# A long convolution with a period of 22912 in place of 23168, ahead of two gated layers

## The chip, the cores and the metric

The kernel runs on one core of a Trainium2 chip. The metric is device time in microseconds (us). Three runs of the kernel before took 1347.17, 1348.60 and 1349.86 us; the median is 1348.6 us.

## The reference

The program computes a long convolution along the sequence, gates it with its input, and sends the result through two feed-forward layers. Cut to what matters:

```python
# x, v: (1, 12480, 128); pos_emb: (12480, 64)
h_filt = (np.maximum(pos_emb @ w1, 0) @ w2) * np.exp(-0.01 * pos)[:, None]
u = x * v
y = irfft(rfft(u, n=2 * S) * rfft(h_filt, n=2 * S))[:S]      # S = 12480, a causal convolution
x = x * y
h = x @ w_in;   x = (h * clip(h + 3, 0, 6) / 6) @ w_out       # d_ff = 2048
h = x @ w_in2;  out = where(h > 0, h, exp(min(h, 0)) - 1) @ w_out2
```

The window `exp(-0.01 n)` is zero in float32 from n = 10398 (`ZERO`) on, so a circular convolution of any period of at least 12480 + 10398 - 1 = 22877 gives the wanted outputs.

## The kernel before, in words

The period is `L = N1 * N2` with `N1 = 180` and `N2 = 128`. A Fourier transform of that length is done in two steps, one along n1 (98 blocks of 128 tokens are not zero) and one along n2; since the data are real, `NK = N1 // 2 + 1 = 91` frequencies along n1 are kept. Everything up to the gate is float32 matrix multiplication against tables that are loaded from memory. In the trace a float32 multiplication appears as two matmul instructions. The work has these stages, one after the other on TensorE (PE):

1. *Hidden filter* (`filter_hidden`, line 278): `pos_emb @ w1`, its two-fold sums into `qb`.
2. *First step* (`first`, lines 320 to 327): 32 blocks of four signal columns and 16 blocks of four filter columns, interleaved two to one. For each block eight multiplications write a PSUM tile `pa` of which 2·NK columns per signal column are used (182 before); the two folds `f` run beside each other on two halves of the output partitions. ScalarE (ACT) evicts each block in one instruction, line 327, into `Au` (a signal half in `qb`, the other in `au`, laid out `(d, k, r)` so that the pitch of one channel is 2·NK elements, 728 bytes) or into `Ar`.
3. *Second step* (lines 378 to 417): the frequencies go in octets of eight (`OCTETS`), eleven full ones and a last one of `NK % 8`, 3 before. For each frequency there is one multiplication `r` (`second_r`), two `h` side by side (`second_h`) and two `z`, one for each half of the channels (`second_u`). VectorE (DVE) then makes two products (line 411) in the buffers `m1` and `m2`, two sets in turn, and GpSimd (POOL) adds them into `Au` (line 416). `z` reads `Au` as its moving operand: 64 pairs of neighbouring floats, one channel pitch apart. Beside this, one job after another of converting int64 weights (lines 198 to 215, over ACT, DVE and POOL) is slipped in by `convert`. The last three octets do their first halves together, then their second halves.
4. *Third step* (`third`, lines 424 to 431): blocks of four channels (the last three of the second half are shorter); eight multiplications each into a PSUM tile `q`, one ACT copy (line 429), two DVE instructions (line 431). The weight operand has NK columns.
5. *Fourth step* (`fourth`, line 504): 33 steps with a table `ti` of NK partitions loaded just ahead (line 472, five buffers), each followed by a DVE product with the signal `xp` (line 549), which had been loaded into `au` in pieces of `EX * 2 * NK` columns (lines 475 to 492).
6. *The two layers* (lines 604 to 698): 25 token tiles of 512, in float32r with a high and a low part, from about 271 us on. This is three quarters of the time.

The order of each engine's instructions is the order in which the code is written; nothing reschedules it. PSUM in stages 1 to 5 is one pool `ps` with two tags, `px` and `py`, of two buffers each (`bank`, line 109). So a new tile waits until the tile two before it under the same tag has been read. Around the step from stage 3 to stage 4 the uses of `py` are, in order: `z` of the last octet's first half, `z` of the last octet but one's second half, the first block of stage 4, the third block of stage 4.

```python
KGROUPS = groups([KC] * (NK // KC) + [NK % KC])       # line 259
OCTETS = groups([OCT] * (NK // OCT) + [NK % OCT])     # line 260
```

Of the kernel before, what the change touches and what calls it, by code (L numbers as in the profile page):

```python
# [9 lines left out]
F32 = mybir.dt.float32  # L10
# [8 lines left out]
S, D, FO, FF = 12480, 128, 64, 2048  # L19

ZERO = 10398
N1, N2 = 180, 128
L = N1 * N2
H1 = -(-S // N2)
NK = N1 // 2 + 1
# [5 lines left out]
HD = D // 2  # L31
# [12 lines left out]
EX = 8  # L44
# [15 lines left out]
def tables():  # L60
    n1, k1, k2 = np.arange(H1), np.arange(NK), np.arange(N2)
    i, m, a = np.arange(HN), np.arange(NM), np.arange(H1) - 2 * SHIFT - 1
    w = 2 * np.pi * (np.outer(n1 - SHIFT, k1) % N1) / N1
    c, s = np.cos(w), np.sin(w)

    t1 = np.stack([np.stack([c, -s], axis=2), np.stack([-s, -c], axis=2)], axis=1)
    k = k1[:, None] + N1 * k2
    w = np.pi * (((2 * i + 1)[:, None, None] * k) % (2 * L)) / L
    gm = np.concatenate([np.cos(w), np.sin(w)], axis=0)

    w = 2 * np.pi * (np.outer(k2, m) % N2) / N2
    c, s = np.cos(w), np.sin(w)
    cs = np.stack([
        np.concatenate([c[:, :HN], s[:, 1:HN], c[:, HN:]], axis=1),
        np.concatenate([c[:, :1], s[:, 1:HN], c[:, 1:]], axis=1),
    ], axis=1)
    ends = (m == 0) | (m == HN)
    w = 2 * np.pi * np.outer(k1, m) / L - np.where(ends, np.pi / 4, 0.0)
    w = 2 * np.pi * (np.outer(k1, a) % N1)[:, None] / N1 + w[:, :, None]
    c = np.outer(np.where((k1 == 0) | (k1 == N1 // 2), 1.0, 2.0) / L, np.where(ends, np.sqrt(0.5), 1.0))  # L80
    ti = np.stack([np.cos(w), -np.sin(w)], axis=2) * c[:, :, None, None]
    window = np.exp(-0.01 * np.arange(S, dtype=np.float32))
    assert not window[ZERO:].any()
    rows = t1 * np.exp(-0.01 * N2 * n1)[:, None, None, None]
    column = np.tile(np.exp(-0.01 * (HN + i)), 2)[:, None]
    ratio = np.tile(np.repeat(RATIO, 2), (H1, 1))
    return [np.ascontiguousarray(z, dtype=np.float32) for z in (t1, gm, cs, ti, rows, column, ratio)]
# [9 lines left out]
def tile_kernel(ctx, tc, xc, vc, xT, posT, w1_d, w2_d, moe_w, t1_d, gm_d, cs_d, ti_d, rows_d, column_d, ratio_d, outT):  # L97
# [21 lines left out]
    AW = 2 * NK * HD  # L119
    RF = FO * N2  # L120

    au = ctx.enter_context(tc.tile_pool(name="aup", bufs=1, side="right")).tile([128, 2 * NK * (HD + EX)], F32, name="au")
    zeros = au[:, -N2:]
    nc.vector.memset(zeros, 0.0)
    bounds = keep.tile([128, 2], F32, name="bounds")
# [326 lines left out]
    ends = range(last - 2, last + 1)  # L452
# [294 lines left out]
```

## Time and profile before

| what | value |
|---|---|
| median of three runs | 1348.6 us (1347.17 to 1349.86) |
| profiled execution, span from first to last instruction | 1346.2 us |
| PE, matmul busy | 1338.7 us, 99% |
| DVE / ACT / POOL busy | 1149.3 / 992.9 / 394.4 us |
| mean granted TensorE clock | 1.000 |

The profiled execution is told by its span alone; its own time is the span and the launch around it, which the page does not time apart. The median of the runs lies 2.4 us above the span. The share of busy PE time is modelled at the ends of instructions, so that a short wait of PE can hide in it; the starts of the engine that reads PE's results, ACT above all, show such a wait better.

### The profile page before, as it was taken

How to read it: one execution, taken by the hardware profiler on the slowest of the kernel's cores; microseconds unless marked ns; L12 is line 12 of the kernel's file. 1: busy time of each engine (PE TensorE's matmuls, PEld its weight loads, DVE VectorE, ACT ScalarE, POOL GpSimd, SP SyncE). 2: the span in 40 equal slices, each digit the busy share in tenths (PEclk: the TensorE clock that was granted, in tenths of full speed). 3: DMA queues.
4: the chain of work that ended last, by engine and by line, in shares of the span. 5: the costliest groups of instructions: out<-in, count | busy, mean ns of one | idle time of the engine just before them, and what ended most of it. 6: DMA issues, size and time to landing. Idle time of an engine off the chain costs nothing.

```text
span 1346.2 us, 20841 instructions
## 1 busy us (share of the span) xinstructions
PE 1338.7 (99%) x8154; PEld 1148.0 (85%) x8154; DVE 1149.3 (85%) x1230; ACT 992.9 (74%) x1171; POOL 394.4 (29%) x280
## 2 busy tenths in 40 slices
PE   9999999999999999999999999999999999999998
PEld 9999999978888888888888888888888888888898
DVE  6749887799988888888888888888888888888897
ACT  5666633288788877788778878887778877887876
POOL 1027721215322222332222232222233222222223
PEclk9999999999999999999999999999999999999999
DMA  8924319730000000000000000000000000000000
GB/s 268 258 75 142 100 34 293 237 106 1 8 0 9 8 9 9 1 8 9 9 0 9 9 9 1 8 9 9 9 1 8 9 9 1 9 8 9 9 3 17
DMA packets 32490, 58.15 MB, mean 43 GB/s; under 512 B 3879, under 2 KB 12168, under 8 KB 32392
## 3 DMA queue, kind: packets, MB, share of 16 engines
q1 hardware_dynamic: 25192, 48.11, 11.7%
q10 hardware_dynamic: 7200, 8.72, 2.0%
q8 instruction: 64, 1.05, 0.3%
q14 instruction: 34, 0.28, 0.1%
HBM read 46.23 MB, written 10.58 MB: 42 GB/s over the span
## 4 chain that ended last, share of the span: by engine, by line
PE 90%; DVE 5%; issue 2%; ACT 1%; POOL 1%; DMA 1%; SPq 0%; POOLq 0%; DVEq 0%; ACTq 0%
PE h L624 37%; PE o L668 37%; PE pa L324 4%; PE q L424 4%; PE y L504 3%; PE z L397 1%; DVE gs L658 1%; PE pr L278 1%; DVE bp L411 1%; DVE qb L411 1%; PE r L378 1%; PE h L387 1%; DVE cv L210 1%; DVE g L645 1%; DMA qb<-in_posT 0%
## 5 line engine op out<-in xcount | busy, mean ns | idle before, releaser
L668 PE MATMUL o<-gs,w 128*128 128x512 f32 (+1 forms) x2400 | 567.1, 384 | 0.5 <-DVE gs L658 0.3
L668 PEld LDWEIGHTS o<-gs,w 128*128 128x128 f32 x2400 | 445.3, 188 | 88.6 <-DVE gs L658 0.8
L637 POOL TENSOR_SCALAR a<-a 128x1024 f32<-128x1024 f32 (+1 forms) x200 | 294.5, 1472 | 720.0 <-ACT a L636 720.0
L658 DVE TENSOR_TENSOR gs<-g,gs 128x1024 fp32r<-128x1024 f32 (+1 forms) x400 | 482.4, 1206 | 4.5 <-ACT gs L653 3.7
L653 ACT CAST gs<-g 128x1024 fp32r<-128x1024 f32 (+1 forms) x400 | 410.2, 1025 | 54.4 <-DVE g L645 52.8
L645 DVE SCALAR_TENSOR_TENSOR g<-a,h 128x1024 f32<-128x1024 f32 (+1 forms) x200 | 238.6, 1193 | 121.4 <-ACT a L634 121.3
L624 PE MATMUL h<-xs,w 128*128 128x512 f32 (+1 forms) x1200 | 302.1, 387 | 0.4 <-DVE g L645 0.4
L624 PE MATMUL h<-x,w 128*128 128x512 f32 (+1 forms) x1200 | 299.0, 385 | 0.2 <-ACT a L636 0.2
L636 ACT ACTIVATE a<-h 128x1024 f32<-128x1024 f32 (+1 forms) x200 | 201.3, 1006 | 92.7 <-PE h L624 91.5
L624 PEld LDWEIGHTS h<-xs,w 128*128 128x128 f32 x1200 | 223.6, 188 | 48.5 <-DVE g L645 1.4
L624 PEld LDWEIGHTS h<-x,w 128*128 128x128 f32 x1200 | 223.0, 188 | 43.8 <-issue 0.5
L634 ACT ACTIVATE a<-h,bounds 128x1024 f32<-128x1024 f32 (+1 forms) x200 | 218.9, 1095 | 51.8 <-PE h L624 51.6
L647 DVE SCALAR_TENSOR_TENSOR g<-a,h 128x1024 f32<-128x1024 f32 (+1 forms) x200 | 237.2, 1186 | 0.2 <-POOL a L637 0.2
L215 POOL TENSOR_TENSOR cv<-cv 128x256 int32<-128x256 int32 x32 | 23.3, 729 | 96.4 <-DVE cv L212 89.8
L416 POOL TENSOR_TENSOR qb<-qb,bp 128x1024 f32<-128x1024 f32 (+2 forms) x14 | 27.7, 1981 | 71.2 <-DMA qb<-in_gm 70.7
L504 PE MATMUL y<-ti,qb 91*64 91x98 f32 (+1 forms) x1024 | 45.9, 247 | 0.8 <-DVE cv L212 0.5
L504 PEld LDWEIGHTS y<-ti,qb 91*64 91x64 f32 x1024 | 45.4, 138 | 1.3 <-DVE cv L212 0.7
L324 PE MATMUL pa<-tab,cv 98*64 98x182 f32 x512 | 44.5, 318 | 0.0
L324 PEld LDWEIGHTS pa<-tab,cv 98*64 98x64 f32 x512 | 37.6, 137 | 3.9
L198 ACT ACTIVATE cv<-cv 128x256 f32<-128x256 f32 x32 | 14.3, 447 | 35.1 <-DMA cv<-in_mw 16.8
L411 DVE TENSOR_TENSOR qb<-z,qb 128x1024 f32<-128x1024 f32 (+2 forms) x15 | 15.9, 1060 | 17.9 <-ACT qb L390 15.2
L431 DVE TENSOR_TENSOR qb<-q,au 91x512 f32<-91x512 f32 (+2 forms) x44 | 26.4, 650 | 3.8 <-ACT au L429 3.8
(67 smaller groups left out, 832.5 us busy)
## 6 DMA issues: line engine op xcount, KB each, us to landing
uv<-in_xc SPq DMA_DIRECT2D x32, 196.0 KB
out_T<-y SPq DMA_DIRECT2D x23, 256.0 KB
au<-in_xT SPq DMA_DIRECT2D x8, 728.0 KB
qb<-in_gm SPq DMA_DIRECT2D x22, 256.0 KB
ti<-in_ti SPq DMA_DIRECT2D x32, 139.3 KB
cv<-in_mw ACTq DMA_DIRECT2D x17, 256.0 KB
uv<-in_vc SPq DMA_DIRECT2D x22, 196.0 KB
w_scratch<-cv ACTq DMA_DIRECT2D x32, 128.0 KB
```

The costliest lines, as they stand in the source:

```text
L324: nc.tensor.matmul(pa[f * HN:(f + 1) * HN, j, :2 * NK], lhsT=src(j, f), rhs=table[:, f], start=True, stop=True)
L424: nc.tensor.matmul(q[:NK, r, j], lhsT=Au[hf][:, s0 + j, :, r], rhs=cs[:, r * N2:(r + 1) * N2], start=True, stop=True)
L504: nc.tensor.matmul(y[h * HD:(h + 1) * HD, off:off + w], lhsT=Q[:NK, h, j // 2, :, j % 2], rhs=ti[:, m - m0, r, H1 - w:], start=r == 0, sto ...
L624: nc.tensor.matmul(h[:, j], lhsT=wslice(2 * m - 2, a, 2 * u + j), rhs=x[:, b], start=i == 0, stop=i == 2)
L634: nc.scalar.activation(a, h, AF.Relu, bias=three)
L636: nc.scalar.activation(a, h, AF.Exp)
L637: nc.gpsimd.tensor_scalar(a, a, 1.0, 0.0, op0=ALU.min, op1=ALU.max)
L645: nc.vector.scalar_tensor_tensor(g, a, 6.0, h, op0=ALU.min, op1=ALU.mult)
L647: nc.vector.scalar_tensor_tensor(g, a, -1.0, h, op0=ALU.add, op1=ALU.max)
L653: nc.scalar.copy(t[:, 0], g)
L658: nc.vector.tensor_tensor(out=t[:, 1], in0=g, in1=t[:, 0].bitcast(F32), op=ALU.subtract)
L668: nc.tensor.matmul(o[:, :WID[t]], lhsT=wslice(2 * m - 1, a, 2 * u + j), rhs=gs[:, b, j], start=u == 0 and j == 0 and i == 0, stop=u == NU ...
```

## The change

`N1` is 179 in place of 180, so the period is 179 · 128 = 22912 and NK is 90 in place of 91. N1 is now odd, so only frequency 0 has no mirror image; the weight of a frequency in `tables` is written for either parity. The buffer `au` is sized by what it must hold beside the frequencies (`S + 4 * N2` = 12992 columns, before 2·91·72 = 13104).

```diff
 ZERO = 10398
-N1, N2 = 180, 128
+N1, N2 = 179, 128
 L = N1 * N2
 H1 = -(-S // N2)
 NK = N1 // 2 + 1
@@
-    c = np.outer(np.where((k1 == 0) | (k1 == N1 // 2), 1.0, 2.0) / L, np.where(ends, np.sqrt(0.5), 1.0))
+    c = np.outer(np.where(2 * k1 % N1 == 0, 1.0, 2.0) / L, np.where(ends, np.sqrt(0.5), 1.0))
@@
-    au = ctx.enter_context(tc.tile_pool(name="aup", bufs=1, side="right")).tile([128, 2 * NK * (HD + EX)], F32, name="au")
+    au = ctx.enter_context(tc.tile_pool(name="aup", bufs=1, side="right")).tile([128, S + 4 * N2], F32, name="au")
```

No instruction changes its place. What changes is shapes and a few counts. On PE, at the end of stage 3 and the start of stage 4 (`r`, `h`, `z` are the multiplications of stage 3, `q` those of stage 4; one row counts multiplications, each of which is two instructions in the trace):

```order
-L378 MATMUL r<-qb 128x128 x11
+L378 MATMUL r<-qb 128x128 x10
 L387 MATMUL h<-qb 128x128 x16
 L397 MATMUL z<-qb 128x128 x8
-L387 MATMUL h<-qb 128x128 x6
-L397 MATMUL z<-qb 128x128 x3
-L397 MATMUL z<-au,qb 128x128 x19
-L424 MATMUL q<-cs,qb 91x128 x128
-L424 MATMUL q<-cs,au 91x128 x128
+L387 MATMUL h<-qb 128x128 x4
+L397 MATMUL z<-qb 128x128 x2
+L397 MATMUL z<-au,qb 128x128 x18
```

One `r`, two `h` and two `z` are gone, all from the last octet, which has two frequencies now; the `q` rows go on with 90 in place of 91. On DVE, at the same place, the products of that octet are shorter and stand where they stood:

```order
-L411 TENSOR_TENSOR qb<-z,qb 128x3x64x2
-L411 TENSOR_TENSOR bp<-z,qb 128x3x64x2
+L411 TENSOR_TENSOR qb<-z,qb 128x2x64x2
+L411 TENSOR_TENSOR bp<-z,qb 128x2x64x2
 L411 TENSOR_TENSOR qb<-z,bp 128x8x64x2
 L411 TENSOR_TENSOR bp<-z,bp 128x8x64x2
 L411 TENSOR_TENSOR qb<-z,qb 128x8x64x2
 L411 TENSOR_TENSOR bp<-z,qb 128x8x64x2
```

In stage 2 all 384 multiplications `pa` have 180 moving columns, and the ACT evictions 720 elements in place of 728. The channel pitch in `Au` is 720 bytes. The 33 loads of `ti` have 90 partitions, the pieces of `xp` are 1440 columns with a last one of 960 (before 1456 and 832), and the last group of the table `gm` has two frequencies in place of three. Stage 6 is the same, instruction for instruction.

## Rows read from the trace of the kernel before

**Rows 1.** The page: busy time of the engines, and the chain that ended last.

```profile
PE 1338.7 (99%) x8154; PEld 1148.0 (85%) x8154; DVE 1149.3 (85%) x1230; ACT 992.9 (74%) x1171; POOL 394.4 (29%) x280
...
PE 90%; DVE 5%; issue 2%; ACT 1%; POOL 1%; DMA 1%; SPq 0%; POOLq 0%; DVEq 0%; ACTq 0%
```

**Rows 2.** Busy time of each engine by stretch, stages 2 to 6.

```profile
core 0: us, PE busy (x) PEld busy (x) DVE busy (x) ACT busy (x) POOL busy (x), PEclk, DMA share, GB/s
19.40:79.00 59.60, 59.60 (x768) 53.64 (x768) 43.51 (x99) 38.32 (x49) 1.16 (x2) 1.00 0.86 242
79.00:168.06 89.06, 88.27 (x912) 84.62 (x912) 69.67 (x87) 56.12 (x77) 57.86 (x36) 1.00 0.32 98
168.06:224.50 56.44, 56.20 (x514) 55.86 (x512) 49.23 (x87) 22.75 (x45) 10.07 (x9) 1.00 0.45 141
224.50:271.00 46.50, 45.90 (x1025) 45.49 (x1025) 33.08 (x78) 12.10 (x29) 12.84 (x16) 1.00 0.80 240
271.00:320.00 49.00, 48.40 (x207) 38.07 (x207) 46.26 (x43) 43.21 (x51) 11.62 (x9) 1.00 0.23 70
320.00:1330.00 1010.00, 1009.75 (x4522) 840.90 (x4521) 888.20 (x801) 803.55 (x850) 292.57 (x198) 1.00 0.02 7
```

**Rows 3.** Timeline of ACT in stage 2: start, length, instruction, [idle before <- releaser].

```profile
22.09 0.78 ACT L327 ACTIVATE qb<-pa 128x728 f32<-128x728 f32 x1 [0.47 <-PE pa L324]
23.67 0.87 ACT L327 ACTIVATE qb<-pa,column 128x728 f32<-128x728 f32 x1 [0.80 <-PE pa L324]
...
79.17 0.78 ACT L327 ACTIVATE au<-pa 128x728 f32<-128x728 f32 x1 [0.46 <-PE pa L324]
```

**Rows 4.** Who waited for whom: us in total, times, longest us.

```profile
ACT qb L327 <- PE pa L324: 14.7, 32, 1.1
...
DVE cv L269 <- PE pa L324: 7.5, 9, 0.9
```

**Rows 5.** Groups by line, stage 3: busy us, mean ns of one | idle before.

```profile
L387 PE MATMUL h<-qb 64*128 64x128 f32 x364 | 24.0, 279 | 0.4 <-ACT qb L379 0.4
L397 PE MATMUL z<-qb 128*128 128x128 f32 x182 | 23.9, 282 | 0.3 <-DVE bp L411 0.3
...
L397 PE MATMUL z<-au,qb 128*128 128x128 f32 x182 | 22.8, 277 | 0.0
L378 PE MATMUL r<-qb 128*128 128x128 f32 x182 | 22.1, 276 | 0.0
```

**Rows 6.** Timeline of ACT, the first five blocks of stage 4.

```profile
170.00 0.58 ACT L429 COPY tab<-q 91x512 f32<-91x512 f32 x1 [5.80 <-PE q L424]
171.75 0.58 ACT L429 COPY au<-q 91x512 f32<-91x512 f32 x1 [1.17 <-PE q L424]
173.64 0.58 ACT L429 COPY au<-q 91x512 f32<-91x512 f32 x1 [1.31 <-PE q L424]
175.43 0.58 ACT L429 COPY tab<-q 91x512 f32<-91x512 f32 x1 [1.21 <-PE q L424]
177.18 0.58 ACT L429 COPY au<-q 91x512 f32<-91x512 f32 x1 [1.17 <-PE q L424]
```

**Rows 7.** Timeline of DVE, the end of stage 3.

```profile
164.68 0.69 DVE L411 TENSOR_TENSOR bp<-z,qb 128x512 f32<-128x512 f32 x1
165.31 0.56 DVE L411 TENSOR_TENSOR qb<-z,qb 128x384 f32<-128x384 f32 x1
...
166.84 1.23 DVE L411 TENSOR_TENSOR qb<-z,bp 128x1024 f32<-128x1024 f32 x1 [0.49 <-POOL qb L416]
...
170.26 1.24 DVE L411 TENSOR_TENSOR bp<-z,qb 128x1024 f32<-128x1024 f32 x1
```

**Rows 8.** Timeline of POOL, the end of stage 3.

```profile
165.52 2.30 POOL L416 TENSOR_TENSOR qb<-qb,bp 128x512 f32<-128x512 f32 x2 [0.24 <-PE z L397]
...
166.76 1.06 POOL L416 TENSOR_TENSOR qb<-qb,bp 128x384 f32<-128x384 f32 x1
```

**Rows 9.** What the DMA queue of SP waited for: us in total, times, longest.

```profile
SPq L472 <- PE y L504: 20.1, 22, 2.2
```

## The prediction

> **What bounds the kernel now.** I read the page first, then the table by stretches, then the timelines of the engines that wait for PE. The page says that PE is busy 99% of the span and carries 90% of the chain that ended last [rows 1]. By stretches it is the same in every stage: 59.60 of 59.60 us in stage 2, 88.27 of 89.06 in stage 3, 56.20 of 56.44 in stage 4, 45.90 of 46.50 in stage 5, and 1009.75 of 1010.00 in most of stage 6; the granted clock is 1.00, the upper of its two levels (2.4 GHz), in all of them [rows 2]. So time can only go where PE's own work goes. But busy PE time has modelled ends, so I check at two places whether a wait of PE hides in it, by the spacing of the ACT instructions that read PE's results.
>
> The change leaves stage 6, three quarters of the span, alone. What it can touch lies before 271 us.
>
> **The change part by part.**
>
> *Stage 2, two columns fewer.* The evictions start at 23.67 and at 79.17 us as the third and the last of 48: 45 intervals in 55.50 us, 1.233 us each [rows 3]. ACT waits for PE before each, and VectorE too waits for PE (7.5 us in 9 waits) to get its buffers back [rows 4], so PE sets this pace and nothing stands close behind it. One interval holds eight pairs of instructions of 182 columns: 154.2 ns a pair. In stage 4 a block is sixteen instructions of 128 columns and takes 1.75 us when undisturbed (175.43 to 177.18) [rows 6], 109.4 ns each. So (154.2 - 109.4) / (182 - 128) = 0.83 ns a column. Two columns of eight pairs are 13.3 ns a block. The third eviction comes 1.58 us after the second [rows 3]: there PE waited for the filter's fold at the start of the stage, so what the first two blocks save is lost in that wait. 46 blocks remain: 46 x 13.3 ns = 0.61 us. Below, the saving could be nothing if an instruction had a floor just under its present length, which the smaller 128-column figure speaks against; above, it can't be more than 48 blocks, 0.64 us. I take 0.61.
>
> The evictions shrink by 8 of 728 elements. ACT waits 0.46 us before most of them [rows 3], so that is worth nothing.
>
> *Stage 3, one frequency fewer.* PE loses two instructions `r`, four `h` and four `z`. By the groups an `r` costs 22.1 / 182 = 121 ns, an `h` 24.0 / 364 = 66, a `z` (23.9 + 22.8) / 364 = 128 [rows 5]: 0.24 + 0.26 + 0.51 = 1.02 us of PE time. Does it reach the end of the stage? The place to look is the beginning of stage 4. Its blocks are evicted at 170.00, 171.75, 173.64, 175.43 and 177.18: 1.75, then 1.89, then 1.79, then 1.75 us apart [rows 6]. The third block came 0.14 us late, although the busy time shows no gap. This block takes the PSUM buffer that the second half of the last octet but one held, and VectorE reads that until 170.26 + 1.24 = 171.50 [rows 7]. The third eviction is 2.14 us after that, a block of 1.75 and the hand-overs at both ends. So PE already arrives there before its buffer is free. What it saves ahead of that place only makes the wait longer.
>
> Then VectorE's work must move. Its four full products there begin at 166.84, after 0.49 us of waiting for POOL [rows 7], for a product buffer that POOL frees when its addition, begun at 165.52, ends at about 166.8 [rows 8]. That addition is the last octet but one's; its input was ready at 164.68 + 0.69 = 165.37 [rows 7]. The short last octet (165.31, 128x384, and its twin) comes between, in VectorE's idle time, and POOL's addition for it (1.06 us from 166.76 [rows 8]) comes after the one that frees the buffer. Shrinking either by a third moves nothing in this chain. So I cost stage 3 at zero. The cover is the chain of products and additions, which keeps step with PE and ends last; were it gone, 1.02 us would come through, less what `r` does under an ACT copy. That is the upper bound; the lower is zero for the counts (another pitch in `Au` is a rival, below).
>
> *The second half's last products* end the stage on VectorE, 128 elements shorter each. The fourth block waits at most 1.79 - 1.75 = 0.04 us there [rows 6], so they give 0 to 0.04; I take 0.
>
> *Stages 4 and 5* keep their counts. The weight columns of stage 4 fall from 91 to 90 and the rows of stage 5 too; PE streams the same moving columns, so 0. The loads of `ti` carry 90 rows, the pieces of `xp` are cut elsewhere, neither is waited for: SP's queue waits 20.1 us for PE to free the `ti` buffers [rows 9], the opposite of a late load. The smaller `au` and the weight in the table are addresses and numbers, 0; they shift no instruction.
>
> **The sum.** Against the profiled execution: 1346.2 - 0.61 = 1345.6 us of span. Around it I leave the 2.4 us by which the median of the runs lies over the span, so 1348.6 - 0.6 = 1348.0 us. The runs scatter over 2.7 us, 0.2%, which is about what a measurement of this kernel can tell from no change; the gain is a quarter of that.
>
> **The rivals.**
>
> *The frequency counts in full.* If the late third block has another cause, PE's 1.02 us comes through: 1348.6 - 0.61 - 1.02 = 1347.0. For it speaks that PE shows 88.27 of 89.06 us busy in the stage [rows 2]; against it the eviction spacing [rows 6].
>
> *Stage 5 waits on transfers after all.* The Trainium skill ("DMA: Bandwidth & Descriptors", section "Why a DMA increments its semaphore by 16 and not by 1") has the number of engines that a transfer uses as the largest divisor up to 16 of its outermost dimension; by it the `ti` loads would go from 13 engines to 15. No row here shows the engines of one load. From the rows alone: transfers take a share of 0.80 in that stage [rows 2], so faster loads could relieve the weight conversion beside them and with it the hand-over into stage 6. All that PE idles there is 46.50 - 45.90 and 49.00 - 48.40, 1.2 us together [rows 2]; if all went, 1348.6 - 0.6 - 1.2 = 1346.8. Against it, SP waits for PE and not PE for loads [rows 9].
>
> *The other side: `z` reads `Au` at a worse pitch.* `z` streams pairs of floats 728 bytes apart, and 720 now. It costs 128 ns where `r`, which streams neighbouring floats, costs 121, and 128 columns at 0.83 ns are 106 [rows 5, 6]. So a pitch may matter. If 720 is worse, the 360 instructions `z` that are left get slower by something between the 7 ns that separate them from `r` and the 22 that separate them from bare columns: 2.5 to 7.9 us on PE, which products and additions cannot hide, since they keep step with it. In the middle, 5.2 us: 1348.6 - 0.6 + 5.2 = 1353.2. It outweighs the gain from 0.61 us / 360 = 1.7 ns an instruction on. A better pitch would give nothing, by the same chain as above. The Trainium skill ("SBUF — State Buffer", section "Door 1: The DMA port swizzle (why `[64,N]` ≈ `[32,N]`)") speaks of 16-byte lines that give full bandwidth when each is hit twice. By that rule both pitches are alike, as a pair of floats on an 8-byte boundary fills half a line either way, and the sum would stay 1348.0; but it would also have `z` as fast as `r`, and the rows have it 7 ns slower.
>
> **How the numbers follow.** The forecast gets 0.80, the full octet 0.07, the transfers 0.04, the pitch 0.05, and 0.04 is left for what I do not see, half to either side. The forecast, the octet and the transfers all lie within 0.2% of before (1345.9 to 1351.3); scatter and the two gains together carry some over the lower edge, 0.05 with the unseen; the pitch, less its low end, and the unseen make 0.06 for slower; 0.89 for the same. The range is the forecast with half the scatter of the runs on either side (1346.6 to 1349.4), stretched to 1346.0 for the two gains and to 1350.5 for the low end of the pitch.
>
> **What would show it.** In the profile after, evictions in stage 2 should be 1.220 us apart, and stage 2 should end 0.6 us sooner. The third block of stage 4 should still be late by more than its neighbours, by about as much as the first two now come sooner, and the distance from the first eviction of stage 2 to the fifth of stage 4 should shrink by 0.6 us and not by 1.6. The mean of `z` should stay at 128 ns. From 271 us on every length should be as before. I would be wrong if `z` changes its pace, if stage 4 starts more than 1 us sooner, or if PE waits anew in stage 5 or at the entry to stage 6.

## The result and the profile after

The changed kernel took 1356.38 us (median of five, 1355.27 to 1357.05), the kernel before 1347.98 in runs beside it: a ratio of 1.0059, interval 1.0047 to 1.0071, 8.4 us slower. 1348.0 had been forecast, with 1350.5 as the upper end. Some executions of these kernels have a mean granted clock of 0.97 or 0.98 of full speed and take 22 to 38 us longer; the ratios and times below leave them out.

The lengths of the stages in the two profiled executions, from the start of the first matmul of each to the first of the next, in us:

| stage | before | after | difference |
|---|---|---|---|
| 1, start to the first `pa` | 19.32 | 19.60 | +0.28 |
| 2, `pa` | 59.74 | 59.13 | -0.61 |
| 3, `r`, `h`, `z` | 88.99 | 94.19 | +5.20 |
| 4, `q` | 56.54 | 56.39 | -0.15 |
| 5, `y` | 46.35 | 46.87 | +0.52 |
| 6, the layers | 1075.26 | 1078.82 | +3.56 |
| span | 1346.2 | 1355.0 | +8.8 |

These are the same stretches after, in the columns of [rows 2]:

```profile
19.60:78.72 59.12, 58.95 (x769) 58.28 (x768) 43.60 (x99) 38.00 (x49) 0.53 (x1) 1.00 0.81 239
78.72:172.91 94.19, 93.47 (x902) 89.92 (x901) 67.32 (x87) 56.12 (x77) 57.30 (x36) 1.00 0.29 92
172.91:229.31 56.40, 56.06 (x515) 55.88 (x513) 48.47 (x86) 22.80 (x45) 9.76 (x9) 1.00 0.45 142
229.31:276.18 46.87, 45.95 (x1025) 45.52 (x1025) 33.11 (x78) 12.13 (x29) 12.05 (x16) 1.00 0.80 236
276.18:1355.00 1078.82, 1074.26 (x4802) 889.88 (x4800) 945.12 (x855) 854.60 (x912) 306.21 (x210) 1.00 0.03 10
```

The clock is granted in full in both. PE is as busy as before: the 5.2 and the 3.6 us come from longer instructions, not from waits. The groups by line and shape say which (after; answers to [rows 5]):

```profile
L668 PE MATMUL o<-gs,w 128*128 128x512 f32 x2208 | 537.6, 391 | 0.1
L624 PE MATMUL h<-xs,w 128*128 128x512 f32 x1104 | 284.8, 394 | 0.4 <-DVE g L645 0.4
L624 PE MATMUL h<-x,w 128*128 128x512 f32 x1104 | 280.0, 389 | 0.0
...
L397 PE MATMUL z<-qb 128*128 128x128 f32 x180 | 27.1, 304 | 0.1
L397 PE MATMUL z<-au,qb 128*128 128x128 f32 x180 | 25.8, 299 | 0.0
```

and the same view of the kernel before, for stage 6:

```profile
L668 PE MATMUL o<-gs,w 128*128 128x512 f32 x2208 | 533.9, 390 | 0.2
L624 PE MATMUL h<-xs,w 128*128 128x512 f32 x1104 | 284.0, 393 | 0.4 <-DVE g L645 0.4
L624 PE MATMUL h<-x,w 128*128 128x512 f32 x1104 | 281.1, 390 | 0.0
```

A `z` takes (27.1 + 25.8) / 360 = 147 ns in place of 128; between the starts of two neighbours in a group (one after the other with the same operands, read from the starts in the traces) the median is 133 ns, before 115. In stage 6 the `o` instructions have taken on 3.7 us, although neither they nor what they read was changed. On PE's timeline of one octet (after), `z<-au` now has 2.23 us from its start to that of `h`:

```profile
101.53 1.95 PE L378 MATMUL r<-qb 128*128 128x128 f32 x16
103.32 2.31 PE L397 MATMUL z<-au,qb 128*128 128x128 f32 x16
105.55 2.06 PE L387 MATMUL h<-qb 64*128 64x128 f32 x32
```

where the kernel before has 1.93, with `r` and `h` as long as now:

```profile
100.66 1.95 PE L378 MATMUL r<-qb 128*128 128x128 f32 x16
102.44 2.00 PE L397 MATMUL z<-au,qb 128*128 128x128 f32 x16
104.37 2.06 PE L387 MATMUL h<-qb 64*128 64x128 f32 x32
```

### The profile page after: what moved, and what is told of

It is laid out like the page before. It is cut to its first block, busy times and chain, and to the rows that moved or that the text cites. A ratio compares the mean times of both kernels' runs of the same rounds, so it can differ in the third digit from the quotient of the medians.

```text
span 1355.0 us, 20821 instructions
## 1 busy us (share of the span) xinstructions
PE 1347.2 (99%) x8144; PEld 1157.8 (85%) x8144; DVE 1147.0 (85%) x1230; ACT 992.4 (73%) x1171; POOL 390.9 (29%) x280
## 4 chain that ended last, share of the span: by engine, by line
PE 93%; DVE 2%; issue 2%; ACT 1%; DMA 1%; POOL 0%; SPq 0%; POOLq 0%; ACTq 0%; DVEq 0%
PE o L668 37%; PE h L624 37%; PE pa L324 4%; PE q L424 4%; PE z L397 4%; PE y L504 3%; PE h L387 2%; PE r L378 1%; DVE gs L658 1%; PE pr L278 1%; DMA w<-w_scratch 1%; DVE g L645 1%; DMA ti<-in_ti 0%; POOL a L637 0%; ACT a L634 0%
## 5 line engine op out<-in xcount | busy, mean ns | idle before, releaser
L416 POOL TENSOR_TENSOR qb<-qb,bp 128x1024 f32<-128x1024 f32 (+2 forms) x14 | 27.1, 1944 | 72.5 <-PE h L387 71.1
L504 PE MATMUL y<-ti,qb 90*64 90x98 f32 (+1 forms) x1024 | 46.0, 247 | 1.3 <-DMA ti<-in_ti 0.8
L504 PEld LDWEIGHTS y<-ti,qb 90*64 90x64 f32 x1024 | 45.5, 138 | 1.8 <-DVE cv L212 1.0
L324 PE MATMUL pa<-tab,cv 98*64 98x180 f32 x512 | 42.7, 316 | 0.0
L431 DVE TENSOR_TENSOR qb<-q,au 90x512 f32<-90x512 f32 (+2 forms) x44 | 26.4, 650 | 4.0 <-ACT au L429 4.0
```

The source lines that it names most:

```text
L324: nc.tensor.matmul(pa[f * HN:(f + 1) * HN, j, :2 * NK], lhsT=src(j, f), rhs=table[:, f], start=True, stop=True)
L504: nc.tensor.matmul(y[h * HD:(h + 1) * HD, off:off + w], lhsT=Q[:NK, h, j // 2, :, j % 2], rhs=ti[:, m - m0, r, H1 - w:], start=r == 0, sto ...
```

## The experiments

**Two causes, taken away one at a time.** `au` lies at the top of the on-chip memory, and the pool `pre` right below it: three quarters of the first layer's input weights (`w0_0` to `w0_2`) and `xs0`, the input tile of every second token tile. A smaller `au` moves these up, by 448 bytes from 13104 to 12992 columns. `au` itself, from which ACT and VectorE cut the input tiles, moves with them; all other tiles of stage 6 stay where they were. So the first suspects were the pitch of 720 bytes for `z` and these addresses for stage 6.

```diff
# e1_wide_au, on the changed kernel; e2_before_small_au: 12992 columns on the kernel before
-.tile([128, S + 4 * N2], F32, name="au")
+.tile([128, 13104], F32, name="au")
# ...
# e3_pitch, on the changed kernel: 91 places a channel, 90 used; e4_pitch_wide_au: both edits
# KP = (91, 91), the places in the two halves; AWS, their sizes
-    Au = [z.rearrange("p (d k r) -> p d k r", r=2, k=NK) for z in (qb[:, 2 * QW - AW:], au[:, :AW])]
+    Au = [z.rearrange("p (d k r) -> p d k r", r=2, k=k)[:, :, :NK] for z, k in zip((qb[:, 2 * QW - AWS[0]:], au[:, :AWS[1]]), KP)]
```

> The changed kernel with au at its old 13104 columns, so that the layer-1 weights and the input tile that lie below au return to their old addresses (448 bytes lower); pitch of Au stays 720 bytes. Theory (two causes: pitch for stage 3, addresses for stage 6): z stays at 133 ns inside a group and stage 3 at 94.2 us, stage 6 (first matmul of the layers to the end of the span) falls from 1078.8 back to 1075.3, the o instructions of layer 1 from 231 to 227 ns; 1352.8 us. Rival (stage 6 is slower because of the moment at which the engines enter it): stage 6 stays at 1078.8 and the time at 1356.4.

It took 1352.95 us, ratio 1.0039 (1.0024 to 1.0054). Stage 3 is still long, stage 6 is as before the change (windows of this run):

```profile
78.76:172.95 94.19, 93.47 (x902) 89.94 (x902) 67.33 (x87) 56.13 (x77) 57.35 (x36) 1.00 0.29 92
275.45:1350.80 1075.35, 1070.72 (x4802) 890.94 (x4800) 944.83 (x855) 854.89 (x912) 309.08 (x210) 1.00 0.03 10
```

> The kernel before (91 frequencies, pitch 728) with au at 12992 columns, so only the addresses below au move up by 448 bytes. Theory (addresses): stage 6 rises from 1075.3 to 1078.8, z stays at 113 to 118 ns, 1351.5 us. Rival (the moment of entry, or the 90 frequencies): nothing changes, 1348.0 us.

1352.13 us, ratio 1.0031 (1.0019 to 1.0043). With 91 frequencies and nothing changed but the size of a buffer, stage 6 is as long as after the change:

```profile
78.20:167.15 88.95, 88.18 (x912) 84.62 (x912) 69.57 (x87) 56.07 (x77) 57.79 (x36) 1.00 0.33 98
269.87:1348.70 1078.83, 1074.30 (x4802) 890.09 (x4800) 945.29 (x855) 854.82 (x913) 306.10 (x210) 1.00 0.03 10
```

> The changed kernel with the channels of Au laid out 728 bytes apart again (90 of 91 places used), all else as changed. Theory (pitch): z falls from 133 to about 114 ns inside a group, stage 3 from 94.2 to about 89.0 us, stage 6 stays at 1078.8; 1351.2 us. Rival (z is slower because its weights lie 512 bytes lower in qb, or because of anything else that came with 90 frequencies): z stays at 133 ns and the time at 1356.4.

1351.26 us, ratio 1.0021 (1.0011 to 1.0032). `z` is back at 115 ns inside a group, and stage 3 at 88.73 us (windows of stages 2 and 3):

```profile
19.29:78.42 59.13, 59.06 (x770) 53.89 (x769) 43.59 (x99) 38.06 (x49) 0.99 (x2) 1.00 0.87 248
78.42:167.15 88.73, 87.32 (x902) 83.77 (x902) 69.06 (x86) 55.56 (x77) 57.47 (x36) 1.00 0.31 98
```

> The changed kernel with both: pitch 728 bytes and au at 13104 columns. Theory (two independent causes): both losses go and what was forecast is left, 0.6 us under the kernel before, 1347.4 us, with evictions of stage 2 at 1.220 us, stage 3 at 89.0 and stage 6 at 1075.3 us. Rival (a third cause): clearly above 1348.

1347.84 us against 1348.24, ratio 0.9998 (0.9987 to 1.0009). With both causes away the time is where it was forecast, but the gain of 0.4 us in the medians can't be told from nothing. In its profile the granted clock is 1.00 in stages 2 to 4 and 0.57 in stage 5; stages 2 and 3 take 59.13 and 88.75 us.

**Which pitch is slow.** The two halves of `Au` can have different pitches, so each run tries two; `au` took other sizes on the way, which gave stage 6 more addresses. These kernels also move the third copy buffer of stage 4 (`QS`) where the wider half needs the room, and the last two do without it.

```diff
+    KP = (92, 95)      # m_92_95: 736 and 760 bytes; m_93_94: 744, 752; m_91_96: 728, 768; m_90_98: 720, 784
```

> The changed kernel with the channels of the first half of Au (read by z<-qb) 736 bytes apart, those of the second half (z<-au) 760, and au at 13192 columns, so that the weights below it lie 288 bytes past a multiple of 512 from the other weights. Theory (a pitch that is a multiple of 16 bytes is slow): z<-qb 133 ns or more inside a group, z<-au 113 to 118. Rival (720 alone is bad): both 113 to 118. Addresses: if only the distance modulo 64 matters, stage 6 lies above 1078; if an offset of 128 is no better than others, anywhere between.

> The changed kernel with the first half of Au 744 bytes apart, the second 752, and au at 13072 columns: the weights below it 256 bytes past a multiple of 512 from the others. Theory (multiples of 16 are slow): z<-qb 113 to 118 ns, z<-au 133. Rival (720 alone): both 113 to 118. Addresses: stage 6 at or below 1075.3 if offsets of 128 and 256 are alike or better, near 1078.8 if not.

> The changed kernel with the first half of Au 728 bytes apart (control), the second 768, au at 13008 columns, and two buffers in place of three for the ACT copies of stage 4. Theory (pairs of floats that fall on few positions modulo some power of two are slow, whatever the width): 768 is a multiple of 256, so z<-au is the slowest of all, above 133 ns inside a group; z<-qb stays at 115. Rival (720 is bad for another reason): z<-au between 112 and 120.

> The changed kernel with the first half of Au 720 bytes apart, as changed, the second 784 (the same remainder modulo 64 as 720), au at 13264 columns, two buffers for the ACT copies. Theory (the remainder modulo 64 decides): both near 133 ns inside a group. Rival (it is 720 itself, or its remainder modulo more than 64): z<-qb 133, z<-au between 112 and 120.

One execution each: 1349.83, 1341.70, 1341.29 and 1343.33 us. The medians inside a group of `z`, with those of the earlier runs:

| pitch, bytes | 720 | 728 | 736 | 744 | 752 | 760 | 768 | 784 |
|---|---|---|---|---|---|---|---|---|
| ns | 133 | 115 | 119 | 112 | 116 | 120 | 112 | 114 |

All three theories on the pitch fell: multiples of 16 are not slow as such (736, 752, 768, 784), nor multiples of 256 (768), nor the remainder 16 modulo 64 (784). 720 is slow by itself among these eight. It is the pitch and not the half or its place: in one and the same program the half at 720 is slow and the one at 784 fast (groups by line and shape of the kernel with 720 and 784):

```profile
L399 PE MATMUL z<-qb 128*128 128x128 f32 x180 | 27.1, 304 | 0.3 <-DVE bp L413 0.3
L399 PE MATMUL z<-au,qb 128*128 128x128 f32 x180 | 22.2, 276 | 0.0
```

Nor is it the address at which a half begins: the one in `au` is slow at 720 with three sizes of `au`, which move its start (133 ns with 12992, 13008 and 13104 columns).

**Which address is good.** The tiles of the pools `wp` and `sb`, weights and buffers further down, are multiples of 2048 bytes, so all of them begin at one remainder modulo 512. The traces hold no addresses: where the distance of the pool `pre` from that remainder is zero is counted from the layout, and the steps between the columns follow from the size of `au`.

| distance modulo 512 | 0 | 64 | 128 | 256 | 288 |
|---|---|---|---|---|---|
| `au`, columns | 13008, 13264 | 12992 | 13104 | 13072 | 13192 |
| stage 6, us | 1069.9 | 1078.8 | 1075.3 | 1069.9 | 1077.1 |

> The kernel before with au at 13008 columns and nothing else: the same distance of a multiple of 512 bytes, 91 frequencies. Theory (distance): stage 6 about 1071.5 us, 1344.5 us. Rival: stage 6 at 1075.3 and 1348.2 us.

1343.81 us, ratio 0.9964 (0.9951 to 0.9977): the kernel before, faster by a buffer that is 96 columns smaller. The gain in stage 6 is 5.4 us, more than the 3.8 that I had expected; most of it comes from `h` of the first layer (284.0 to 280.1 us), about 1 us each from `o` and `h` of the second (this run):

```profile
L668 PE MATMUL o<-gs,w 128*128 128x512 f32 x2208 | 532.7, 389 | 0.4 <-ACT y L597 0.4
L624 PE MATMUL h<-xs,w 128*128 128x512 f32 x1104 | 280.1, 390 | 0.5 <-DVE g L645 0.5
L624 PE MATMUL h<-x,w 128*128 128x512 f32 x1104 | 280.1, 389 | 0.0
```

> The changed kernel, pitch 720, with au at 13008 columns and nothing else. Theory (two independent causes that add): stage 3 stays at 94.2 us, stage 6 falls from 1078.8 to 1069.9, 1356.4 - 9.0 = 1347.4 us. Rival (the slow z of stage 3 also delays the entry to stage 6): above 1349.

1347.88 us beside 1347.98, ratio 0.9994 (0.9984 to 1.0004). Stage 3 is as long as in the changed kernel, stage 6 as short as in the run before (windows of this run): the two causes add, and the changed kernel with 16 columns more in `au` is no slower than the kernel before.

```profile
78.46:172.67 94.21, 93.49 (x901) 89.96 (x901) 67.31 (x87) 56.13 (x77) 57.40 (x36) 1.00 0.29 92
277.42:1347.40 1069.98, 1065.04 (x4801) 890.29 (x4800) 945.13 (x855) 854.66 (x912) 309.27 (x210) 1.00 0.03 10
```

**Which of the moved tiles.** With pitch 728, a gap of 64 bytes between the weights and `xs0` moves one of the two: with `au` at 13008 columns it pushes the weights 64 bytes down from the good distance and leaves `xs0`; with 12992 the weights are back and `xs0` lies 64 bytes too high.

```diff
+    pre.tile([128, 16], F32R, name="gap")        # t_x_shifted with au at 12992, t_w_shifted at 13008
     xs = [pre.tile([128, 2, TT], F32R, name="xs0")]
```

> Pitch 728, the three weight tiles above at the good distance (a multiple of 512 bytes from the buffers below), and only the input tile xs0, used by every second token tile, moved by 64 bytes. Theory (what collides is the weight read and the moving read of neighbouring instructions, by the distance of the two tiles): stage 6 between the good 1069.9 and the 1078.8 of a shift of both, about 1073 us, since half of the token tiles are untouched. Rival (only the weight tiles matter): 1069.9. Rival (only xs0 matters): 1078.8.

> Pitch 728, xs0 at the good distance, and only the three weight tiles above moved by 64 bytes. Theory (distance of weight read and moving read): six of eight units of every token tile are touched, so more than with xs0 alone: about 1076 us in stage 6. Rival (only xs0 matters): 1069.9. Rival (only the weight tiles matter): 1078.8.

Moving the weights alone gave 1346.42 us and 1071.6 in stage 6, 1.7 more than without. `h` took 1.9 us more, `o` nothing. The total of the run that moved `xs0` alone, 1386.72 us, says nothing, since its granted clock was 0.56 in stage 5; but from the start of token tile 2 to the end the clock is 1.00. That stretch in this run, in the one with nothing moved (`b_best`, below) and in the changed kernel, where both are moved:

```profile
355.04:1384.80 1029.76, 1025.75 (x4603) 853.45 (x4602) 898.50 (x814) 813.16 (x865) 297.00 (x202) 1.00 0.02 7
318.06:1340.73 1022.67, 1018.67 (x4603) 853.26 (x4602) 900.87 (x814) 813.15 (x865) 299.58 (x202) 1.00 0.02 7
323.37:1354.98 1031.61, 1027.57 (x4603) 853.38 (x4602) 900.35 (x814) 813.25 (x865) 295.43 (x202) 1.00 0.02 7
```

So `xs0` alone costs 7.1 us and both together 8.9. The effect shows in single units too: the first of the even token tile 12, which reads `xs0`, and the first of tile 13, which does not (PE's timeline of this run):

```profile
793.50 1.55 PE L627 MATMUL h<-xs,w 128*128 128x512 f32 x6
794.89 2.93 PE L671 MATMUL o<-gs,w 128*128 128x512 f32 x12
...
799.02 1.32 PE L627 MATMUL h<-xs,w 128*128 128x512 f32 x5
...
837.66 1.52 PE L627 MATMUL h<-xs,w 128*128 128x512 f32 x6
839.02 2.88 PE L671 MATMUL o<-gs,w 128*128 128x512 f32 x12
...
843.10 1.52 PE L627 MATMUL h<-xs,w 128*128 128x512 f32 x6
```

From one `h<-xs` to the next, tile 12 takes 5.52 us and tile 13 5.44, the length with nothing moved, though `au` begins 64 bytes off here too; so it is not the place of `au` that counts. The `o` that follow an `h` with the moved `xs0` are slow (12 in 2.93 us, 2.88 otherwise), although they read `gs` and other weights; by their starts the first ten of the twelve are. So both tiles count, the input tile four times as much, and what it does to PE lasts beyond the instructions that read it. The expected order of the two (weights worse) was wrong. Nor is it the distance of the weights from the input tile alone: that is 64 bytes more in both kernels, and only one slows `o`.

**The best version.**

> The changed kernel with pitch 728 and au at 13008 columns, so that the three weight tiles and the input tile below au lie at a multiple of 512 bytes from the weights and buffers below. Theory (the pace of stage 6 depends on this distance): the h instructions of layer 1 that read those tiles fall from 230 to the 224 ns of the h instructions of layer 2, and o of layer 1 stays at 227; stage 6 from 1075.3 to about 1071.5, with the forecast's 0.6 us 1344.0 us. Rival (an offset of 128 already has all that there is): 1347.7 us.

1342.77 and 1342.23 us, ratio 0.9958 (0.9940 to 0.9975), under the 1344.0 expected because stage 6 came down to 1069.9 us and not 1071.5. `h` and `o` are at the lengths of the run with 91 frequencies and 13008 columns; stage 3 takes 88.75 us.

> The changed kernel with both halves of Au 744 bytes apart, the pitch with the fastest z so far (112 ns inside a group), and au at 13008 columns. Theory (stage 3 ends with the products and additions, so a faster z than at 728 gives nothing): stage 3 stays within 0.2 us of the 88.75 us that pitch 728 gave, 1342.5 us. Rival (z sets the stage): 360 x 2.5 ns = 0.9 us less, 1341.6 us.

Four runs from 1340.87 to 1342.90 us, ratio 0.9947 (0.9933 to 0.9962). Its interval overlaps those of pitch 728 and of the kernel before with 13008 columns, so the frequency itself is not shown to be worth anything even here. Stage 3, at a granted clock of 1.00 in its profile, takes 88.44 us for 88.75: `z` faster by 2 to 3 ns an instruction, 0.8 to 1.1 us in all, gave 0.3. That lies between the two expectations; most of the gain went into waits.

## Why the prediction was wrong

Two terms that the sum put at nothing cost time: the pitch of `z` in stage 3, 5.2 us, and the smaller `au` in stage 6, 3.56 us. With the 0.61 us gained in stage 2 and under 1 us in the other stages they make the 8.8 us of span.

*Stage 2, right.* 59.74 to 59.13 us is the 0.61 forecast. The third and the last eviction after:

```profile
23.93 0.86 ACT L327 ACTIVATE qb<-pa,column 128x720 f32<-128x720 f32 x1 [0.83 <-DMA uv<-in_xc]
...
78.83 0.77 ACT L327 ACTIVATE au<-pa 128x720 f32<-128x720 f32 x1 [0.45 <-PE pa L324]
```

54.90 us over 45 intervals are 1.220 each, as forecast for 1.233 before [rows 3].

*Stage 3, the frequency at zero: right, once the pitch is taken out.* With pitch 728 and 90 frequencies (e3), stage 3 is 0.26 us shorter and stage 4 0.22 us longer, 145.49 us together for 145.53. And the third block of stage 4 is late by 2.11 - 1.75 = 0.36 us, where it was 0.14 [rows 6]: PE arrives sooner and waits longer, for VectorE to free the buffer (ACT's timeline, and the group of `q` with the 0.2 us that PE idles for VectorE, none before).

```profile
169.09 0.58 ACT L431 COPY tab<-q 90x512 f32<-90x512 f32 x1 [6.17 <-PE q L426]
170.84 0.58 ACT L431 COPY au<-q 90x512 f32<-90x512 f32 x1 [1.17 <-PE q L426]
172.95 0.58 ACT L431 COPY au<-q 90x512 f32<-90x512 f32 x1 [1.53 <-PE q L426]
...
L426 PE MATMUL q<-cs,qb 128*90 128x128 f32 x256 | 28.3, 273 | 0.2 <-DVE bp L413 0.2
```

In the changed kernel the sign that I had named for this is missing: the third block comes 1.74 us after the second, not late at all. The slow `z` has used up the cover.

```profile
176.61 0.58 ACT L429 COPY au<-q 90x512 f32<-90x512 f32 x1 [1.17 <-PE q L424]
178.35 0.58 ACT L429 COPY au<-q 90x512 f32<-90x512 f32 x1 [1.17 <-PE q L424]
```

*The pitch, the failed choice.* It was the rival given 0.05: 2.5 to 7.9 us, 5.2 in the middle, and stage 3 grew by 5.2. That the middle was hit is luck. It stood for 14.5 ns an instruction; `z` took 128.9 ns in e3 (the lines below) and 147 here, so 18 ns or 6.5 us more in all, and of that stages 3 and 4 show 5.1 us (150.58 for 145.49). The other 1.4 us did not lengthen the stages: the slow `z` took the place of waits, of which the late third block is one. So "which products and additions cannot hide" was not right either.

```profile
L399 PE MATMUL z<-qb 128*128 128x128 f32 x180 | 23.7, 282 | 0.3 <-DVE bp L413 0.3
L399 PE MATMUL z<-au,qb 128*128 128x128 f32 x180 | 22.7, 278 | 0.4 <-DVE bp L413 0.4
```

What should have told me: `z` cost 7 ns more than `r` on the same columns [rows 5], so the cost of a strided read was seen, and nothing in the trace bounded it at another stride. One chance in twenty was too little. The Trainium skill ("SBUF — State Buffer", section "Door 1: The DMA port swizzle (why `[64,N]` ≈ `[32,N]`)"), which speaks of 16-byte lines, would have both pitches alike; the runs have 133 and 115 ns, so here the measurement decides against it.

*The smaller `au` at zero: the step that failed unseen.* What I had put down as "addresses and numbers, 0" cost 3.56 us, no rival named it, and "Stage 6 is the same, instruction for instruction" was true and not enough. That the addresses alone do it is shown both ways (e1, e2). The kernel before had the sign of it: `h<-xs` took 284.0 us and `h<-x` 281.1, with the same shapes and counts. I had read only instructions that the change touches.

*Stage 5.* PE now waits for a table once, which I had named as a sign of being wrong:

```profile
238.79 37.46 PE L504 MATMUL y<-ti,qb 90*64 90x98 f32 x872 [0.81 <-DMA ti<-in_ti]
```

In the ten profiles with 90 rows and a granted clock of 1.00 throughout, the stage takes 45.4 to 48.9 us, and in seven of them PE waits for a `ti` load, 0.2 to 2.5 us in all; in the three with 91 rows it takes 45.6 to 46.4 us, and PE waits for none. That points to the 90 rows, but three profiles are few and no run changed the loads alone: whether the 0.5 us here belong to the change or to scatter is open. A gain from the loads does not show.

## What to carry to other kernels

A change that only takes work away can still move a stride or an address; list which strides and which tile addresses it alters, as one lists instructions, and hold a price for each open, even where the shapes and order are the same. Where one engine carries the time, compare instructions of one shape on different tiles: a difference of a few ns between them is a loss that an address may give back (5.4 us here, for a change of one buffer's size). A saving on that engine ahead of a place where another one ends last turns into a wait (in e3 PE had 1.02 us less work, and stages 3 and 4 together were 0.04 us shorter); the spacing of the instructions that read its results shows this where busy time does not.

## What the runs showed of the hardware

A float32 matmul that reads its moving operand as pairs of floats took 112 to 120 ns at seven pitches from 728 to 784 bytes and 133 at 720. Why 720 is open: no remainder that was tried explains it. A matmul of 512 float32r columns took 227 ns where it reads no moved tile ((839.02 - 837.66) / 6, tile 13 above), and 232 with the input tile 64 bytes off the distance at which the other tiles lie ((794.89 - 793.50) / 6, tile 12). Of the five distances modulo 512 that were tried, 0 and 256 give the shortest stage 6; 64, 128 and 288 don't. Why the distance counts, and how the slowness passes on to the next instructions, which read other tiles, is open as well.
